# Decay attention and mixer on one core: the first channel group's outputs of batch 2 by seven products

## The chip, the cores and the metric

The kernel runs on one core of one Trainium2 chip. The metric is the device time of one execution in microseconds (us). The engines are TensorE (PE in the profile; its weight loads are PEld), VectorE (DVE), ScalarE (ACT), GpSimd (POOL) and SyncE (SP), which here only issues DMAs.

## The reference

`x` is the output of a block-wise decay attention (4 batches, 8 heads, 768 positions, 64 dims per head; blocks of 64), laid out as 4 x 768 x 512. A mixer follows, and only its second half, the channel mixer, is touched by the change:

```python
xt = x.transpose(0, 2, 1)
h = np.maximum(xt @ w_tok1, 0.0) @ w_tok2
u = x + h.transpose(0, 2, 1)
h2 = np.maximum(u @ w_ch1, 0.0) @ w_ch2      # w_ch1 512 x 1536, w_ch2 1536 x 512
return (u + h2)
```

All is fp32. The weights arrive as 8-byte floats and are narrowed on the chip. Each fp32 operand of a product is held as a high part in a rounded fp32 form that the matmul takes, and a low part that is the rest. A product of two operands is three matmuls: high by high, low by high and high by low.

## The kernel before

**Channel groups and units.** The 1536 hidden channels are cut into six groups of 256 (`NG = 6`, `g` from 0 to 5). A unit is one group for one batch; there are 24, numbered by `n`. Units 0 to 11 do batches 0 and 1 with the groups going up, units 12 to 23 do batches 2 and 3 with the groups going down. Two of the last are swapped (L775), so the last four are: unit 20 = group 1, batch 2; unit 21 = group 0, batch 2; unit 22 = group 1, batch 3; unit 23 = group 0, batch 3. In this text a unit's *pass* is the call `run(n, ...)`, which issues the hidden products of unit n together with the output products of unit n - 1.

**Hidden products.** For a unit, the 256 x 512 weights times the 512 x 768 batch is done by seven block products in place of eight, m1 to m7, each of six matmuls (two row tiles by the three high and low terms) that stream 384 columns. Two functions do this. `mixing` (L809) ends in the four hidden blocks 11, 12, 21, 22 after the relu, each split in a high and a low part. `mixing_seven` (L866) forms, beside blocks 11, 22 and 21, four sums and differences T1 to T4 of hidden blocks, and splits all seven; these are the operands of an output by seven products. Its last pieces (`rest[n]`, function `u`, L931) run in the next pass, behind m1.

**Output products.** `out_pair` (L1014) does a quarter of a unit's output by plain block products, 12 matmuls; four of them, 48 matmuls, make a unit's output, and four DVE additions of 128 x 768 put it into the batch's tile `uT`. `out_seven` (L968) does a unit's output by seven products M1 to M7 of six matmuls, 42 in all, each followed by a DVE addition of 128 x 768 into `uT`. M1, M6, M7 and M4 accumulate one after another in one pair of PSUM banks, M5, M3 and M2 in another; so each of M6, M7, M4, M3 and M2 starts only when the addition of the one before it in its pair is done.

**Weights of the output by seven.** `out_seven` needs seven combinations of the four blocks of the group's w_ch2 rows. `load_sums(g)` (L944) brings the group's fp32 w_ch2 (512 KB) from a copy in DRAM, and `sum_steps(g)` (L952) makes the combinations: four splits (ACT rounds the high part, POOL subtracts for the low part) and four DVE additions of 128 x 256. The fp32 copies in DRAM are written while groups 1 to 4 first pass (`save_c2`). Of group 0, `save(0)` has stored all six tiles, the high and the low part of its w_ch2 among them (`saved[0][4]` and `saved[0][5]`), and `restore(0, 1)` (L1087) brings these two back for `out_pair`.

**Which unit does what.** `SEVEN` (L777) lists the units that use `mixing_seven` and `out_seven`: units 14 to 20 and 22. Group 0 is left out, so units 21 and 23 use `mixing` and `out_pair`.

**What sets the order.** The order on every engine is the order in which the program issues. `run` goes through a list of slots (`SLOTS_OF`, L1107 on) and between slots issues side work that `background(n)` lists with due times: a slot of a product counts 6, a slot of an `out_pair` 12, so a pass is 84 to 90 long. The side work in question is the loading of sums, the sum steps, the restoring of weights, and `store(b, x)` (L1028): one quarter of a batch's output, two DVE transposes of 128 x 384 into a tile `y`, and eight DMAs of 48 KB on SP's queue. Each engine takes its instructions strictly in order, so an instruction that waits holds all that stand behind it.

**The end.** After pass 23 come `out_pair(23, 0)` and `out_pair(23, 1)`, two stores of batch 3 by DVE transposes (tile `ylast`, 14 DMAs on SP's queue and two on ACT's), and four last sums (`last_sum`) whose blocks PE transposes back (`finish`, L1049) and ACT's queue stores in three DMAs of 384, 192 and 192 KB.

Of the kernel before, what the change touches and what calls it, by code (L numbers as in the profile page):

```python
# [22 lines left out]
def kernel(  # L23
# [750 lines left out]
    units = [(g, b) for g in range(NG) for b in (0, 1)] + [(g, b) for g in reversed(range(NG)) for b in (2, 3)]  # L774
    units[-3], units[-2] = units[-2], units[-3]  # L775
    NU = len(units)
    SEVEN = [n for n in range(FIRST, NU - 1) if units[n][0] > 0]  # L777
    hs = {}
    scratch, rest = {}, {}
    late = {}  # L780
# [163 lines left out]
    def load_sums(g):  # L944
        pool, tag = (upool, "uT0") if g == NG - 2 else (hidp, "hh0")
        late["raw", g] = pool.tile([P, JG * DM], U32, tag=tag, name=f"sums_raw{g}")
        nc.sync.dma_start(out=sum_raw(g), in_=saved_c2[g])

    def sum_raw(g):
        return late["raw", g]  # L950
# [77 lines left out]
    def store(b, x, between=None):  # L1028

        sh, t = x // 2, 2 * (x % 2)  # L1030
        k = 2 * b + sh
        y = ytags[0]
        ytags.rotate(-1)
        if isinstance(y, str):
            y = hidp.tile([P, 1024], F32, tag=y, name=f"y{k}{t}")
        y = y[:, : 2 * SB]
        y = y.rearrange("p (blk t q) -> p blk t q", t=2, q=32)
        ub = uT[b][:, t : t + 2, sh * SB : (sh + 1) * SB]
        to = out[b, sh * SB : (sh + 1) * SB].rearrange("(blk s) (t q c) -> q s blk t c", s=32, t=4, q=4)
        for tt in (t, t + 1):  # L1040
            nc.vector.transpose(out=y[:, :, tt - t, :], in_=ub[:, tt - t])
            if between and tt == t:
                between()
        for m in range(4):
            for tt in (t, t + 1):
                eng = nc.scalar if k == LAST - 1 and tt == 3 and m >= 2 else nc.sync
                eng.dma_start(out=to[m, :, :, tt], in_=y[m * 32 : (m + 1) * 32, :, tt - t])
# [39 lines left out]
    def restore(g, x):  # L1087
        if x == 0:
            weights[g] = group_tiles(f"r{g}", g % 2, c2=False)
        else:  # L1090
            both = c2_tile(f"r{g}", g % 2)
            weights[g] += [both[:, 0], both[:, 1]]
        for y in range(6)[4 * x : 4 + 2 * x]:
            nc.sync.dma_start(out=flat(weights[g][y]).bitcast(F32), in_=saved[g][y])
# [19 lines left out]
    def background(n):  # L1114
# [4 lines left out]
        def add(when, *fs):  # L1119
            ev.extend((when, f) for f in fs)  # L1120
# [17 lines left out]
        if 1 < n < NP1 - 1:  # L1138
            to = g + 1
            if n % 2 == 0:  # L1140
                if n == 2:
                    pc = piece_steps(2)
                    add(6, *pc, lambda: fetch(2, 0), split_c2(weights[1], 2, narrowed[2]))
                pa = piece_steps(3)
                add(12, pa[0], pa[1], pa[2])
                add(24, pa[3], pa[4])
                if n < NP1 - 2:
                    add(24, lambda: fetch(to, 1))
                add(36, split_c2(weights[g], 3, narrowed[3]))
                if g < NG - 1:  # L1150
                    add(48, lambda: save_c2(g))
                if n < NP1 - 2:
                    pb = piece_steps(0)
                    weights[to] = group_tiles(to, to % 2)
                    steps["c1"] = c1 = split_c1(weights[to], narrowed[0], narrowed[1], nc.vector)
                    add(36, pb[0])
                    add(48, pb[1], pb[2])
                    add(72, pb[3], pb[4], lambda: fetch(to, 2))
                    add(84, c1[0])
            else:  # L1160
                c1, pa, pb = steps["c1"], piece_steps(1), piece_steps(2)
                add(6, pa[0], pa[1], pa[2])
                add(12, pa[3], pa[4], c1[1], lambda: fetch(to, 3))
                add(36, c1[2], c1[3], c1[4], c1[5], c1[6])
                add(48, c1[7], pb[0], pb[1], pb[2])
                add(72, pb[3], pb[4], split_c2(weights[to], 2, narrowed[2]))
                if to < NG - 1:
                    add(72, lambda: fetch(to + 1, 0))
                if to - 1 < NG - 2:
                    add(84, lambda: save(to - 1))  # L1170
# [42 lines left out]
        if n == FIRST:  # L1213
# [1 line left out]
            add(6, ss[0], ss[1])  # L1215
            add(48, *ss[2:7])
            add(60, ss[7])
        if FIRST <= n < NU - 5 and n % 2 == 0:
            add(84, lambda: load_sums(g - 1))
        if FIRST < n <= NU - 4:  # L1220
            if n % 2:
                late["steps"] = ss = sum_steps(g - 1)
                add(48, ss[0], ss[1])
            else:
                ss = late["steps"]
                add(36, *ss[2:7])
                add(42, ss[7])
        if n >= NU - 2:
            x = 2 * (n - NU + 2)
            add(36, lambda: store(2, x))  # L1230
            add(84, lambda: store(2, x + 1))
        if n >= NP1 + 2 and n % 2 == 0 and n // 2 - NG <= NG - 2:
            nxt = g - 1
            add(6, lambda: restore(nxt, 0))
        if n == NU - 3:
            add(12, lambda: restore(0, 1))
        return deque(sorted(ev, key=lambda x: x[0]))

    second = {}
# [70 lines left out]
```

## Time and profile before

| what | value |
|---|---|
| time before | 563.82 us median of 3 runs (563.75 to 564.18) |
| the profiled execution's own time | 563.57 us |
| span in its profile | 561.6 us, mean granted TensorE clock 0.995 |
| PE busy | 544.1 us, 97% of the span |
| DVE, POOL, ACT busy | 433.4, 271.6, 244.2 us |
| pass 20 (units 20 and 19) | 483.90 to 498.59 us |
| pass 21 | 498.59 to 513.31 us |
| pass 22 | 513.31 to 529.18 us |
| pass 23 | 529.18 to 543.90 us |
| outputs of unit 23 and the last stores | 543.90 to 561.6 us |

The passes' limits are the starts of the first matmul of each m1. A row of the profile's timeline gives start, length, engine, line of the kernel, operation, output <- inputs, shapes and count, and in brackets how long the engine stood idle before it and what ended that. Rows with SPq or ACTq are the issuing of DMAs; the lists of DMAs give size and the time from issue to landing. Matmuls overlap, so their spacing, not the 0.34 us of one, is what one costs.

### The profile page before, as it was taken

The numbers are of one execution on the slowest core, as the hardware profiler recorded it, in microseconds if no ns is written. First come the engines' busy times: TensorE is split into PE (matmuls) and PEld (weight loads), VectorE is DVE, ScalarE is ACT, GpSimd is POOL, SyncE is SP. The second block draws the span as 40 slices with busy tenths as digits, with TensorE's granted clock in tenths as the row PEclk, the third lists the DMA queues.
The fourth block names the chain that finished last, engine by engine and source line by source line (L and its number), as shares of the span: only waits on it lengthen the run. The fifth ranks groups of instructions, "written<-read, shape, count | busy, mean of one in ns | idle before, by whom it ended". The sixth has DMA issues, their size and how long they took to land.

```text
span 561.6 us, 10781 instructions
## 1 busy us (share of the span) xinstructions
PE 544.1 (97%) x4186; PEld 529.2 (94%) x4186; DVE 433.4 (77%) x650; ACT 244.2 (43%) x490; POOL 271.6 (48%) x248
## 2 busy tenths in 40 slices
PE   5999998999999999999999999999999999999994
PEld 4888887999999999999999999999999999999994
DVE  4786789598787989887878887888678777785683
ACT  3564442336253554343444344353455545442421
POOL 5666452557214464443444454453466656662330
PEclk9999999999999999999999999999999999999998
DMA  9998999999102433351725300015864131320337
GB/s 185 253 205 198 211 166 182 188 190 155 28 2 82 176 119 131 104 215 40 246 73 210 109 1 1 0 29 75 212 113 136 57 114 57 113 76 0 45 49 133
DMA packets 176019, 65.72 MB, mean 117 GB/s; under 512 B 163552, under 2 KB 166752, under 8 KB 175968
## 3 DMA queue, kind: packets, MB, share of 16 engines
q1 hardware_dynamic: 172224, 63.75, 47.8%
q10 hardware_dynamic: 3744, 1.28, 0.9%
q8 instruction: 33, 0.54, 0.4%
q14 instruction: 18, 0.15, 0.1%
HBM read 48.24 MB, written 16.78 MB: 116 GB/s over the span
## 4 chain that ended last, share of the span: by engine, by line
PE 82%; DVE 6%; SPq 5%; DMA 4%; ACT 1%; issue 1%; DVEq 0%; ACTq 0%
PE po L1007 23%; PE pa L794 12%; PE pc L794 9%; PE pb L794 7%; PE pa L981 6%; PE pc L981 5%; PE ph L451 4%; PE pd L794 3%; SPq L111 3%; PE sc L299 2%; PE xT L323 2%; DMA vn<-in_v_dram 2%; PE pu L488 2%; PE pu L471 1%; PE xT L333 1%
## 5 line engine op out<-in xcount | busy, mean ns | idle before, releaser
L1022 DVE TENSOR_TENSOR uT<-po,uT 128x768 f32<-128x768 f32 x62 | 58.9, 952 | 22.6 <-PE po L1007 22.3
L286 POOL COPY stb<-sv 64x320 f32<-64x320 f32 x32 | 26.8, 838 | 45.0 <-DVE sv L273 44.1
L805 ACT ACTIVATE c<-c 128x384 f32<-128x384 f32 x42 | 22.1, 526 | 59.2 <-DVE c L850 33.4
L987 DVE TENSOR_TENSOR uT<-pa,uT 128x768 f32<-128x768 f32 x32 | 30.6, 956 | 11.0 <-PE pa L981 10.3
L323 PE MATMUL xT<-a,vn 128*64 128x128 f32 x384 | 35.7, 277 | 0.0
L340 ACT COPY uT<-xT 128x384 f32<-128x384 f32 x32 | 15.3, 478 | 46.2 <-PE xT L333 46.2
L807 POOL TENSOR_TENSOR h22l<-c,h22h 128x384 fp32r<-128x384 f32 x14 | 14.4, 1030 | 41.6 <-ACT h22h L806 41.6
L307 DVE TENSOR_TENSOR a<-sc,mask 128x768 f32<-128x768 f32 x32 | 29.0, 948 | 5.1 <-PE sc L299 5.1
L333 PE MATMUL xT<-qs,stb 128*64 128x128 f32 x320 | 31.3, 273 | 0.0
L987 DVE TENSOR_TENSOR uT<-pc,uT 128x768 f32<-128x768 f32 x24 | 22.9, 955 | 10.6 <-PE pc L981 10.6
L375 POOL TENSOR_TENSOR c1l<-cs,c1h 128x512 fp32r<-128x512 f32 x15 | 19.2, 1292 | 23.2 <-ACT c1h L374 23.2
L451 PE MATMUL ph<-xhi,w1h 128*128 128x256 f32 x96 | 28.2, 294 | 1.3 <-DVE sv L273 0.9
L1007 PE MATMUL po<-h12h,c 128*128 128x384 f32 x112 | 28.7, 337 | 0.0
L1007 PE MATMUL po<-h11h,c 128*128 128x384 f32 x112 | 28.6, 336 | 0.0
L1007 PE MATMUL po<-h21h,c 128*128 128x384 f32 x112 | 28.6, 336 | 0.0
L1007 PE MATMUL po<-h22h,c 128*128 128x384 f32 x112 | 28.6, 336 | 0.0
L451 PE MATMUL ph<-xhi,w1l 128*128 128x256 f32 x96 | 27.1, 282 | 0.0
L451 PE MATMUL ph<-xlo,w1h 128*128 128x256 f32 x96 | 27.1, 282 | 0.0
L299 PE MATMUL sc<-qT,kT 64*128 64x128 f32 x384 | 26.4, 285 | 0.2 <-ACT qT L237 0.2
L299 PEld LDWEIGHTS sc<-qT,kT 64*128 64x128 f32 x384 | 23.4, 192 | 3.3 <-issue 1.8
L364 DVE TENSOR_TENSOR xlo<-xp,xhi 128x384 fp32r<-128x384 f32 x32 | 17.6, 552 | 11.2 <-ACT xhi L363 11.0
L252 POOL TENSOR_TENSOR qs<-qT,lamp 128x640 f32<-128x640 f32 x16 | 25.2, 1577 | 0.3
(401 smaller groups left out, 1928.8 us busy)
## 6 DMA issues: line engine op xcount, KB each, us to landing
raw<-in_moe_w_ch_dram SPq DMA_DIRECT2D x20, 512.0 KB, 3.8
vn<-in_v_dram SPq DMA_DIRECT2D x16, 384.0 KB, 5.2
kn<-in_k_dram SPq DMA_DIRECT2D x30, 192.0 KB, 5.4
out_dram<-y SPq DMA_DIRECT2D x96, 48.0 KB, 1.9
qn<-in_q_dram SPq DMA_DIRECT2D x44, 96.0 KB, 3.9
kr<-in_k_dram SPq DMA_DIRECT2D x32, 96.0 KB, 2.8
dc1h<-c1h SPq DMA_DIRECT2D x4, 768.0 KB, 5.4
dc1l<-c1l SPq DMA_DIRECT2D x4, 768.0 KB, 6.8
```

The costliest lines, as they stand in the source:

```text
L252: nc.gpsimd.tensor_mul(out=qss[i], in0=qTs[i][:, P:].rearrange("p (c i) -> p c i", i=P), in1=lamp[:, p, None, :].broadcast_to([P, NC - 1, P]),
L286: nc.gpsimd.tensor_copy(out=st[r, :, h, :], in_=sv[r].rearrange("p (e c) -> p c e", c=NC - 1))
L299: nc.tensor.matmul(out=sc[h][:, c * P : (c + 1) * P], lhsT=kTs[i][r, cs], rhs=qTs[i][r, cs], start=True, stop=True,)
L307: nc.vector.tensor_mul(out=a, in0=pair.rearrange("p h (c i) -> p h c i", i=P), in1=mask[:, 2 * p : 2 * p + 2, None, :].broadcast_to([P, 2, ...
L323: nc.tensor.matmul(out=xT[h * D : (h + 1) * D, cs], lhsT=vns[i][:, h, c, :], rhs=weights_of[i, g, h][:, cg, :], start=(cg == 0), stop=False,)
L333: nc.tensor.matmul(out=xT[h * D : (h + 1) * D, cs], lhsT=st[:, c - 1, h, :], rhs=qss[i][:, c - 1, :], start=False, stop=(cg == 2),)
L451: nc.tensor.matmul(out=ph, lhsT=w[:, c, fs], rhs=x[:, c], start=(i == 0), stop=(i == 3 * NC - 1))
L794: nc.tensor.matmul(out=to, lhsT=w[:, t], rhs=x[:, t], start=(start and i == 0), stop=(i == 5), skip_group_check=not start,)
L981: nc.tensor.matmul(out=pair[x][:, t], lhsT=w[:, t], rhs=h, start=(start and i == 0), stop=(i == 2), skip_group_check=not start,)
L987: nc.vector.tensor_add(out=ub, in0=pair[x], in1=ub)
L1007: nc.tensor.matmul(out=to, lhsT=w[:, jj, t * P : (t + 1) * P], rhs=h, start=(i == 0), stop=(i == 3 * JG - 1))
L1022: nc.vector.tensor_add(out=ub, in0=po, in1=ub)
```

## The change

Unit 21 joins the units that work by seven products (`SEVEN` is now units 14 to 22). Its hidden products go through `mixing_seven`, its output, in pass 22, through `out_seven`.

The combinations of group 0's w_ch2 need its fp32 values, of which no copy is kept. `load_sums(0)` loads the stored high and low parts, 512 KB each, and a new step `whole` adds them on DVE (128 x 1024). In pass 21 stand `whole` and all four splits and four additions of the sum steps. The high and low parts themselves are still wanted for unit 23, and `restore(0, 1)` moves from pass 21 to pass 23, since its tile now holds the low parts of group 0's combinations until pass 22 is over. Batch 2's four stores change order and place: the two quarters of its second half go first, in pass 22, and the two of its first half follow in pass 23, earlier in the pass than the two that stood there.

```diff
-    SEVEN = [n for n in range(FIRST, NU - 1) if units[n][0] > 0]
+    SEVEN = range(FIRST, NU - 1)
...
     def load_sums(g):
         pool, tag = (upool, "uT0") if g == NG - 2 else (hidp, "hh0")
         late["raw", g] = pool.tile([P, JG * DM], U32, tag=tag, name=f"sums_raw{g}")
-        nc.sync.dma_start(out=sum_raw(g), in_=saved_c2[g])
+        if g == 0:
+            late["lows"] = hidp.tile([P, JG * DM], F32, tag="hl0", name="sums_lows")
+            nc.sync.dma_start(out=sum_raw(0).bitcast(F32), in_=saved[0][4])
+            nc.sync.dma_start(out=late["lows"], in_=saved[0][5])
+        else:
+            nc.sync.dma_start(out=sum_raw(g), in_=saved_c2[g])
+
+    def whole():
+        raw = sum_raw(0).bitcast(F32)
+        nc.vector.tensor_add(out=raw, in0=raw, in1=late["lows"])
...
-        if FIRST <= n < NU - 5 and n % 2 == 0:
+        if FIRST <= n < NU - 3 and n % 2 == 0:
             add(84, lambda: load_sums(g - 1))
+        if n == NU - 3:
+            ss = sum_steps(g)
+            add(6, whole, ss[0], ss[1])
+            add(48, *ss[2:7])
+            add(60, ss[7])
...
         if n >= NU - 2:
-            x = 2 * (n - NU + 2)
-            add(36, lambda: store(2, x))
-            add(84, lambda: store(2, x + 1))
+            x, when = ((2, (48, 72)), (0, (12, 48)))[n - NU + 2]
+            add(when[0], lambda: store(2, x))
+            add(when[1], lambda: store(2, x + 1))
...
-        if n == NU - 3:
-            add(12, lambda: restore(0, 1))
+        if n == NU - 1:
+            add(6, lambda: restore(0, 1))
```

A condition on `save_c2` gains a `0 <`; the step it guards was never reached for group 0.

The order on DVE where pass 20 goes over into pass 21, before. `uT_63` and `uT_62` are the tiles of batches 3 and 2, `pa` and `pc` PSUM banks, `scratch_*` fp32 temporaries of the hidden products; L987 is the addition behind an output product, L924 and L933 are the last differences of the unit before:

```order
L987 TENSOR_TENSOR uT_63<-pa_5611,uT_63 128x2x384
L924 TENSOR_TENSOR scratch_c<-scratch_c,scratch_a_4711 128x384
L933 TENSOR_TENSOR t_20_5768<-scratch_d,scratch_c 128x384
L987 TENSOR_TENSOR uT_62<-pa_5759,uT_62 128x2x384
L832 TENSOR_TENSOR scratch_b_4716<-pb_5788,scratch_a_4712 128x384
L987 TENSOR_TENSOR uT_62<-pc_5758,uT_62 128x2x384
```

And now (L996 is the former L987, L956 is `whole`):

```order
L996 TENSOR_TENSOR uT_63<-pa_5611,uT_63 128x2x384
L924 TENSOR_TENSOR scratch_c<-scratch_c,scratch_a_4711 128x384
L933 TENSOR_TENSOR t_20_5775<-scratch_d,scratch_c 128x384
L956 TENSOR_TENSOR sums_raw_5755<-sums_raw_5755,sums_lows 128x1024
L996 TENSOR_TENSOR uT_62<-pa_5766,uT_62 128x2x384
L894 TENSOR_TENSOR scratch_a_4712<-pb_5797,scratch_a_4712 128x384
L996 TENSOR_TENSOR uT_62<-pc_5765,uT_62 128x2x384
```

`whole` stands between the last difference of unit 20 and the addition behind M1 of pass 21.

The end of SP's queue, before (`y` are the stores of batch 2, `c2r` the restored parts of group 0's w_ch2, `ylast` the stores of batch 3):

```order
L1094 DMA c1hr_5633<-dc1h_2728 128x1536
L1094 DMA c1lr_5634<-dc1l_2729 128x1536
L1094 DMA c2r_5785<-dc2h_2730 128x1024
L1094 DMA c2r_5785<-dc2l_2731 128x1024
L1047 DMA out_dram<-y_5942 32x12x32 x8
L1047 DMA out_dram<-y_6020 32x12x32 x8
L1047 DMA out_dram<-y_6100 32x12x32 x8
L1047 DMA out_dram<-y_6184 32x12x32 x8
L1047 DMA out_dram<-ylast_6195 32x12x32 x14
```

And now:

```order
L1103 DMA c1hr_5633<-dc1h_2728 128x1536
L1103 DMA c1lr_5634<-dc1l_2729 128x1536
L949 DMA sums_raw_5755<-dc2h_2730 128x1024
L950 DMA sums_lows<-dc2l_2731 128x1024
L1056 DMA out_dram<-y_5985 32x12x32 x8
L1056 DMA out_dram<-y_6030 32x12x32 x8
L1103 DMA c2r_6082<-dc2h_2730 128x1024
L1103 DMA c2r_6082<-dc2l_2731 128x1024
L1056 DMA out_dram<-y_6092 32x12x32 x8
L1056 DMA out_dram<-y_6149 32x12x32 x8
L1056 DMA out_dram<-ylast_6219 32x12x32 x14
```

The two loads for `whole` take the restored parts' place, and the restored parts come between the two stores of pass 22 and the two of pass 23.

On PE, behind m1 of pass 22, stood the first of 48 matmuls by `out_pair`; there stands M1 now, six of the 42 by `out_seven`. Before, and now:

```order
L1007 MATMUL po_5901<-h11h_5809,c2r_5785 128x384 x2
L1007 MATMUL po_5901<-h11l_5810,c2r_5785 128x384
L1007 MATMUL po_5901<-h21h_5862,c2r_5785 128x384 x2
L1007 MATMUL po_5901<-h21l_5863,c2r_5785 128x384
L1007 MATMUL po_5901<-h11h_5809,c2r_5785 128x384 x2
```

```order
L990 MATMUL pa_5909<-h11h_5806,sums_5764 128x384
L990 MATMUL pa_5909<-h11h_5806,c2s_5762 128x384
L990 MATMUL pa_5909<-h11l_5807,sums_5764 128x384
L990 MATMUL pa_5909<-h11h_5806,sums_5764 128x384
L990 MATMUL pa_5909<-h11h_5806,c2s_5762 128x384
L990 MATMUL pa_5909<-h11l_5807,sums_5764 128x384
```

In pass 22 the operands are now `sums` and `c2s`, the high and low combinations that pass 21 makes, where they were the restored parts `c2r`.

More of the change, by code (lines that the diff above doesn't have):

```diff
@@ L1149, in background @@
                 add(36, split_c2(weights[g], 3, narrowed[3]))
-                if g < NG - 1:
+                if 0 < g < NG - 1:
                     add(48, lambda: save_c2(g))
```

## The prediction

> **What bounds the kernel now.** I read the page's share of busy time first, then the busy time by pass, then the end of the span.
>
> ```profile
> PE 544.1 (97%) x4186; PEld 529.2 (94%) x4186; DVE 433.4 (77%) x650; ACT 244.2 (43%) x490; POOL 271.6 (48%) x248
> ```
>
> Busy time of each engine by pass (PE, PEld, DVE, ACT, POOL with their counts, then granted clock, DMA share, GB/s), for passes 20 to 23 and the rest:
>
> ```profile
> 483.90:498.59 14.69, 14.69 (x85) 14.69 (x85) 11.85 (x19) 7.65 (x18) 9.45 (x9) 1.00 0.29 107
> 498.59:513.31 14.72, 14.72 (x85) 14.72 (x85) 11.09 (x16) 5.42 (x13) 6.99 (x7) 1.00 0.21 73
> 513.31:529.18 15.87, 15.87 (x91) 15.87 (x91) 8.17 (x12) 5.14 (x11) 3.20 (x4) 1.00 0.18 26
> 529.18:543.90 14.72, 14.72 (x85) 14.72 (x85) 12.16 (x19) 5.45 (x12) 6.81 (x7) 1.00 0.37 54
> 543.90:561.60 17.70, 10.41 (x61) 9.32 (x60) 8.47 (x14) 2.21 (x5) 1.02 (x1) 0.84 0.64 112
> ```
>
> PE is busy through all four passes without a gap at a granted clock of 1.00, so what PE has to do sets the time up to 543.90, and DVE, the next, has 2.5 to 7.7 us to spare in a pass. The last stretch is another matter: PE is busy for 10.4 of 17.7 us. The issues and landings there, first SP's queue, then DVE's transposes for its last two stores, then the last DMA of either queue with its time to landing, then what closes the program:
>
> ```profile
> 537.17 3.94 SPq L1047 DMA_DIRECT2D out_dram<-y  x8
> 545.57 4.82 SPq L1047 DMA_DIRECT2D out_dram<-y  x8
> 550.49 8.76 SPq L1047 DMA_DIRECT2D out_dram<-ylast  x14
> ...
> 547.21 1.04 DVE L1041 STREAM_TRANSPOSE ylast<-uT 128x384 f32<-128x384 f32 x2
> 549.33 0.58 DVE L1041 STREAM_TRANSPOSE ylast<-uT 128x384 f32<-128x384 f32 x1
> 550.28 0.56 DVE L1041 STREAM_TRANSPOSE ylast<-uT 128x384 f32<-128x384 f32 x1
> ...
> 558.75 0.49 SPq L1047 DMA_DIRECT2D out_dram<-ylast  x1
> out_dram<-ylast SPq DMA_DIRECT2D x1, 48.0 KB, 1.9
> 555.75 0.38 ACTq L1067 DMA_DIRECT2D out_dram<-ylast  x1
> out_dram<-ylast ACTq DMA_DIRECT2D x1, 192.0 KB, 2.9
> ...
> L1306 SPq DRAIN  x3: 7/7/7, 560.9 to 561.2; - x3
> ```
>
> SP's last DMA lands at 558.75 + 1.9 = 560.65, ACT's at 555.75 + 2.9 = 558.65; SP drains at 560.9, 0.95 us after its last landing the span is over. So SP's queue ends the kernel, 2.0 us behind ACT's, though the page's chain of waits follows PE and DVE to 555.7. And SP is late because it is still issuing batch 2's last quarter: its eight DMAs run from 545.57 to 550.39, and batch 3's first transpose is ready near 547.21 + 0.58 = 547.8.
>
> **The change part by part.** *PE.* Unit 21's hidden products stay seven of six matmuls. Its output falls from 48 to 42. What six matmuls cost, from the chain of waits:
>
> ```profile
> 538.81 1.05 PE pa L981 x6
> ```
>
> So -1.05 us in pass 22, all of it on the path.
>
> *The loads for `whole`.* They take the place of the restored parts, the same two 512 KB copies, of which the profile has issue and time to landing. They wait for tile `hh0`, that is for POOL's last reading of group 1's sums:
>
> ```profile
> 498.61 0.32 SPq L1094 DMA_DIRECT2D c2r<-dc2h  x1
> 498.97 0.43 SPq L1094 DMA_DIRECT2D c2r<-dc2l  x1
> c2r<-dc2l SPq DMA_DIRECT2D x1, 512.0 KB, 4.4
> 493.33 2.55 POOL L375 TENSOR_TENSOR c2s<-sums_raw,sums_odd 128x512 fp32r<-128x512 f32 x2 [2.27 <-ACT sums_odd L374]
> ```
>
> POOL is through at 495.88, the second load is issued 0.36 us later and lands 4.4 us after that, near 500.65. Group 0's other weights stand ahead of them on SP's queue and went out by 483.9, so nothing holds them; behind them stand only pass 22's stores, not due before 520.
>
> *`whole` and the lock.* DVE reaches `whole` when L933 ends. What is around it on DVE and POOL, and PE's M6 of pass 21:
>
> ```profile
> 500.32 0.56 DVE L933 TENSOR_TENSOR t<-scratch_d,scratch_c 128x384 f32<-128x384 f32 x1
> 500.92 0.96 DVE L987 TENSOR_TENSOR uT<-pa,uT 128x768 f32<-128x768 f32 x1
> 500.84 1.02 POOL L884 TENSOR_TENSOR late_t<-scratch_c,late_t 128x384 fp32r<-128x384 f32 x1 [1.10 <-ACT late_t L883]
> 501.82 1.02 POOL L884 TENSOR_TENSOR h21l<-scratch_d,h21h 128x384 fp32r<-128x384 f32 x1
> 503.86 0.34 PE L981 MATMUL pa<-late_t,sums_odd 128*128 128x384 f32 x1
> ...
> 491.26 0.41 DVE L548 TENSOR_TENSOR sums_raw<-sums_raw 128x256 f32<-128x256 f32 x1
> ```
>
> 128 x 256 takes 0.41 us, 128 x 384 0.56: 0.15 for 128 more, so 128 x 1024 comes to 0.56 + 5 x 0.15 = 1.3 us. Taken alone that would end at 502.2, M1's addition at 503.1, and M6 at 503.86 would not notice. But DVE operations with both inputs in SBUF do not run beside POOL's subtractions:
>
> ```profile
> 526.96 1.01 POOL L884 TENSOR_TENSOR h22l<-scratch_c,h22h 128x384 fp32r<-128x384 f32 x1 [4.29 <-ACT h22h L883]
> 527.42 0.97 DVE L919 TENSOR_TENSOR scratch_a<-scratch_b,scratch_a 128x384 f32<-128x384 f32 x1 [0.66 <-ACT scratch_b L916]
> ...
> 412.33 1.01 POOL L884 TENSOR_TENSOR late_t<-scratch_c,late_t 128x384 fp32r<-128x384 f32 x1 [1.04 <-ACT late_t L883]
> 412.58 1.18 DVE L933 TENSOR_TENSOR t<-scratch_d,scratch_c 128x384 f32<-128x384 f32 x1
> 413.31 1.33 POOL L884 TENSOR_TENSOR h21l<-scratch_d,h21h 128x384 fp32r<-128x384 f32 x1
> ```
>
> L919 ends 0.42 us after POOL does, whenever it started; so does L933, and there the POOL operation behind it waits in turn. One at a time, then, in turns, the blocked one 0.14 us shorter than usual from the release. POOL's L884 starts at 500.84, a hair ahead of `whole`: `whole` runs from 501.86 to about 503.0, M1's addition, which stands behind it, to 503.9, and M6 stands at the edge: a stall of 0 to 0.15 us. If `whole` wins the race instead, none.
>
> [...]
>
> *The other sum steps.* Four DVE additions (4 x 0.42) and four POOL subtractions join pass 21, which on DVE goes from 11.1 to about the 11.85 us of pass 20 plus 1.3. Pass 20 has the same additions and two of the splits, and PE has no gap there, so their bare time is covered. They stand behind M3's addition now, where pass 20 has them ahead of it in 1.1 us of idle time, so DVE's L919 (497.55 in pass 20, 512.3 one pass on) may come as late as 513.2. There the lock adds a second delay: POOL's last sums subtraction, put off like its operands, falls on L919, and T1's subtraction on L924. A meeting costs DVE at most one POOL operation, 1.0 to 1.3 us (2.55 for two above). Behind L924 stand the cast of T2 on ACT and, in ACT's strict order, the copy of m1's bank for which m6 of the next pass waits. In pass 20 these are
>
> ```profile
> 485.97 0.47 ACT L889 COPY scratch_a<-pa 128x384 f32<-128x384 f32 x1
> 488.10 0.34 PE L794 MATMUL pa<-T2h,c1hr 128*128 128x384 f32 x1
> ```
>
> 1.7 us of air. A lateness of 0.9 and one whole meeting, 2.2, overruns it by 0.5; a second of half the length makes 1.0. With the 0.15 at M6, PE's stalls in passes 21 and 22 lie between 0, if POOL and DVE hardly meet, and 1.2 us. I take 0.4, one meeting of less than full length. PE then gains 1.05 - 0.4 = 0.65 us.
>
> The cover of the new ACT casts (four of 0.4 to 0.6 us) is ACT's idle half; without it they would cost 2.2.
>
> *The stores.* In pass 22 and 23 batch 2's quarters leave earlier. The last, due at 48 of 84, gives SP its eight DMAs near 538, as the store at 537.17 above, done by about 543. SP is then free when batch 3's transposes come. These stay tied to PE's output products, so they come 0.65 us sooner: first transpose done at 547.21 + 0.58 - 0.65 = 547.1. With the pace of today, 8.76 us for 14 issues, the last DMA starts 0.49 before 555.9 and lands at 557.3. ACT's chain, moved by 0.65 only, lands at 558.0, and becomes the end. Its last 192 KB took 2.9 us amid SP's issues (the one before 3.6). With SP through by then it will be shorter; loads of 128 KB took 2.0 to 2.5 us in this kernel, by these rows:
>
> ```profile
> a11hr<-da11h SPq DMA_DIRECT2D x1, 128.0 KB, 2.0
> a11hr<-da11h SPq DMA_DIRECT2D x1, 128.0 KB, 2.5
> ```
>
> Bounds 2.1 and 3.6; I take 2.5, which is -0.4.
>
> The restored parts, now behind M4 of pass 22 (near 528), land under 5 us later by the rows above, 9 us ahead of their use at about 543; pass 23's stores, queued behind them, are due after 531. DVE's transposes in passes 22 and 23 are the same eight, and these passes have DVE room as the table shows (8.2 and 12.2 of 15); three more additions of 0.96 bring pass 22 to about 13 of 14.7.
>
> *The sum*, on the profiled execution's own 563.57: PE -0.65; the end from SP's queue to ACT's, 560.65 to 558.65, -2.0; the shorter last landing -0.4. That is 560.5. The median of the runs stands 0.25 above the profiled execution, so **560.8 us**.
>
> **The rivals.** *Late `whole`.* If the second load lands after 501.8, POOL's next subtraction gets in first and `whole` ends a further 1.0 us later; M6 stalls by 1.0 to 1.2 and PE gains nothing. For it: the margin is 1.1 us on a landing of 4.4. Against: the same copies, in as idle a stretch. The end still gains 2.0 to 2.4: 561.4 to 562.
>
> *The end stays.* If the DMA engines, not SP's issuing, pace the last stores, moving the stores ahead frees nothing. For it: the DMA share of 0.64 over the last stretch, issues that stretch from 0.49 to over 0.6 us. Against: before 545.57 SP and DMAs stand idle again, and the eight issues at 537.17 went out at 0.49 each. Only PE's 0.65 would be left: 563.2.
>
> *No lock at this place.* `whole` wins its race and POOL and DVE pass each other: the whole 1.05, 560.4.
>
> *Slower.* `whole` waits at the head of DVE's queue, so every us by which its loads land after 501.8 goes to PE. It costs 1:1, and has to eat 1.05 + 2.4 and 1.1 more to be seen as a loss: a landing after 506, some 10 us after the issue, against 4.4 for its like. The time would be 565 or more.
>
> That the change doesn't do what it says is ruled out by the order, six matmuls fewer on PE.
>
> **How the numbers follow.** Forecast 0.72, no lock 0.06, late `whole` 0.11, the end stays 0.08, slower 0.03. The forecast's own ends: stalls 0 and landing 2.1 give 563.57 + 0.25 - 1.05 - 2.0 - 0.8 = 560.0; stalls 1.2 and landing 3.2 (nearly the mean of 2.9 and 3.6) give 563.57 + 0.25 + 0.15 - 2.0 + 0.3 = 562.3. With a little below for SP's and ACT's ends that I place to 0.1 or 0.2 only: 559.8 to 562.3, which holds the late case too. A change under 0.2%, 1.1 us, can't be told from none here: faster 0.89, same 0.08, slower 0.03.
>
> **What would show it.** Right: M1 to M7 of pass 22 in place of 48 L1007 matmuls; `whole` near 1.1 us past POOL's L884, or 2.1 long with the wait counted; PE gaps in passes 21 and 22 of 0.2 to 0.6 us in sum; SP's `ylast` issues from about 547 without a stretch of `y` ahead; the last landing ACT's. Wrong: a wait of `whole` on a DMA; 14 issues that take over 9 us; a gap ahead of unit 23's outputs for the restored parts.

## The result, and the profile after

The changed kernel takes 561.21 us (median of 5 runs, 560.80 to 561.38) against 563.82 before: a ratio of 0.9949, 95% interval 0.9937 to 0.9961. The forecast was 560.8 with a range of 559.8 to 562.3. The profiled execution has a time of its own of 561.38 us and a span of 559.5, where before it was 563.57 and 561.6.

The page of the changed kernel, busy time of the engines, six PE instructions fewer:

```profile
PE 542.8 (97%) x4180; PEld 527.9 (94%) x4180; DVE 439.2 (78%) x659; ACT 248.3 (44%) x500; POOL 281.5 (50%) x256
```

Busy time by pass in the changed kernel, for passes 21, 22 and 23 and the rest (PE, PEld, DVE, ACT, POOL with their counts, granted clock, DMA share, GB/s):

```profile
498.58:513.30 14.72, 14.72 (x86) 14.72 (x85) 12.37 (x19) 7.92 (x18) 11.42 (x11) 1.00 0.11 42
513.30:528.08 14.78, 14.78 (x86) 14.65 (x85) 12.56 (x19) 6.40 (x14) 8.66 (x8) 1.00 0.12 17
528.08:542.80 14.72, 14.72 (x86) 14.72 (x86) 13.29 (x21) 5.88 (x13) 6.99 (x7) 1.00 0.79 151
542.80:559.50 16.70, 10.41 (x61) 9.32 (x60) 7.53 (x12) 2.21 (x5) 1.01 (x1) 0.90 0.58 106
```

Pass 22 takes 14.78 us where it took 15.87, and the last stretch 16.70 where it took 17.70. These two, 1.09 and 1.00, are the 2.1 us between the spans of these two executions. Pass 21, which now has `whole` and the sum steps, is as long as before, and POOL's work in it grew from 6.99 to 11.42 us.

`whole` (L956) and its neighbours, first on DVE, then on POOL:

```profile
500.31 0.56 DVE L933 TENSOR_TENSOR t<-scratch_d,scratch_c 128x384 f32<-128x384 f32 x1
500.78 1.22 DVE L956 TENSOR_TENSOR sums_raw<-sums_raw,sums_lows 128x1024 f32<-128x1024 f32 x1
501.92 0.95 DVE L996 TENSOR_TENSOR uT<-pa,uT 128x768 f32<-128x768 f32 x1
...
500.82 2.06 POOL L884 TENSOR_TENSOR late_t<-scratch_c,late_t 128x384 fp32r<-128x384 f32 x1 [1.10 <-ACT late_t L883]
```

In this execution `whole` waits for no DMA and runs at once, 1.22 us. POOL's subtraction is the one that is held: 2.06 us where the like took 1.02. M1's addition (L996), one input of which is in PSUM, takes its usual 0.95 us beside the second half of that.

The two later meetings of DVE and POOL in passes 21 and 22, and the only gap of PE there:

```profile
508.07 0.95 DVE L548 TENSOR_TENSOR sums_raw<-sums_raw 128x256 f32<-128x256 f32 x1
513.03 0.56 DVE L919 TENSOR_TENSOR scratch_a<-scratch_b,scratch_a 128x384 f32<-128x384 f32 x1
513.62 1.54 DVE L921 TENSOR_TENSOR scratch_b<-scratch_c,scratch_b 128x384 f32<-128x384 f32 x1
...
507.72 1.02 POOL L884 TENSOR_TENSOR h11l<-scratch_a,h11h 128x384 fp32r<-128x384 f32 x1
513.09 1.65 POOL L375 TENSOR_TENSOR c2s<-sums_raw,sums 128x512 fp32r<-128x512 f32 x1
...
517.50 0.42 PE L794 MATMUL pa<-T2h,c1hr 128*128 128x384 f32 x1
517.76 0.34 PE L794 MATMUL pa<-T2h,c1lr 128*128 128x384 f32 x1
```

L548 lasts 0.95 instead of 0.41, L921 1.54 instead of 0.56: DVE loses 0.54 and 0.98 us. On PE the second matmul of m6 starts 0.26 us after the first, where 0.175 is the usual spacing, so 0.08 us is all that reaches it.

The end: SP's issues of batch 3 as one stretch, then its second and its last issue alone, then ACT's last, the landings of the last of either queue, and the close of SP's program:

```profile
546.72 10.60 SPq L1056 DMA_DIRECT2D out_dram<-ylast  x14
547.17 1.91 SPq L1056 DMA_DIRECT2D out_dram<-ylast  x1
556.84 0.47 SPq L1056 DMA_DIRECT2D out_dram<-ylast  x1
554.64 0.44 ACTq L1076 DMA_DIRECT2D out_dram<-ylast  x1
out_dram<-ylast SPq DMA_DIRECT2D x1, 48.0 KB, 1.9
out_dram<-ylast ACTq DMA_DIRECT2D x1, 192.0 KB, 3.3
L1320 SPq DRAIN  x3: 7/7/7, 558.8 to 559.1; - x3
```

SP has no `y` left when batch 3 begins, and starts at 546.72 instead of 550.49. But its 14 issues take 10.60 us instead of 8.76, one of them 1.91. Its last DMA lands at 556.84 + 1.9 = 558.74, ACT's at 554.64 + 3.3 = 557.94. SP still ends the kernel, by 0.8 us instead of 2.0.

### The profile page after: what moved, and what is told of

It is laid out like the page before. It is cut to its first block, busy times and chain, and to the rows that moved or that the text cites. A ratio compares the mean times of both kernels' runs of the same rounds, so it can differ in the third digit from the quotient of the medians.

```text
span 559.5 us, 10806 instructions
## 1 busy us (share of the span) xinstructions
PE 542.8 (97%) x4180; PEld 527.9 (94%) x4180; DVE 439.2 (78%) x659; ACT 248.3 (44%) x500; POOL 281.5 (50%) x256
## 4 chain that ended last, share of the span: by engine, by line
PE 82%; DVE 7%; SPq 4%; DMA 3%; ACT 2%; issue 1%; DVEq 0%; ACTq 0%
PE po L1016 22%; PE pa L794 12%; PE pc L794 9%; PE pb L794 7%; PE pa L990 7%; PE pc L990 5%; PE ph L451 4%; PE pd L794 3%; SPq L111 3%; PE sc L299 2%; PE xT L323 2%; PE pu L488 2%; PE xT L333 2%; PE pu L471 1%; DMA qn<-in_q_dram 1%
## 5 line engine op out<-in xcount | busy, mean ns | idle before, releaser
L1031 DVE TENSOR_TENSOR uT<-po,uT 128x768 f32<-128x768 f32 x58 | 55.2, 952 | 17.4 <-PE po L1016 17.1
L996 DVE TENSOR_TENSOR uT<-pa,uT 128x768 f32<-128x768 f32 x36 | 34.4, 954 | 11.0 <-PE pa L990 10.3
L996 DVE TENSOR_TENSOR uT<-pc,uT 128x768 f32<-128x768 f32 x27 | 25.8, 954 | 12.0 <-PE pc L990 12.0
```

The source lines that it names most:

```text
L996: nc.vector.tensor_add(out=ub, in0=pair[x], in1=ub)
L1031: nc.vector.tensor_add(out=ub, in0=po, in1=ub)
```

## The experiments

**Which part brings the time.** The change without its earlier stores in pass 23:

```diff
-            x, when = ((2, (48, 72)), (0, (12, 48)))[n - NU + 2]
+            x, when = ((2, (48, 72)), (0, (36, 84)))[n - NU + 2]
```

> The changed kernel with batch 2's two stores of pass 23 back at the times they had before (36 and 84 in place of 12 and 48). Theory A, SP's queue sets the end and the moved stores freed it: the last eight DMAs of batch 2 run from about 544.5 to 549.3, the 14 issues behind them start near 549.4 instead of 546.7, last landing near 559.7 in place of 558.7, about 1 us slower than the changed kernel, near 562.2. Theory B, the last stores are paced by the DMA engines and their start does not matter: as the changed kernel, near 561.2.

Measured: 562.71 us, ratio 0.9976 (0.9967 to 0.9985). The other way round, the kernel before with the stores of pass 23 at the early places and nothing else:

```diff
-            x = 2 * (n - NU + 2)
-            add(36, lambda: store(2, x))
-            add(84, lambda: store(2, x + 1))
+            x, when = ((0, (36, 84)), (2, (12, 48)))[n - NU + 2]
+            add(when[0], lambda: store(2, x))
+            add(when[1], lambda: store(2, x + 1))
```

> The kernel before with only the stores of pass 23 moved from 36 and 84 to 12 and 48; unit 21 stays with out_pair. Theory A: PE as before, SP's last 14 issues start near 547.8 instead of 550.5 and take 8.8 to 10.6 us, ACT's last landing (558.65) is the floor; 0.9 to 2.0 us off, 561.8 to 562.9. Theory B: no change, 563.8.

Measured: 562.61 us, ratio 0.9974 (0.9963 to 0.9984). The parts bring 0.24% and 0.26% and add up to the 0.51% of the whole. So about half of the gain is the six matmuls and half the stores; the profile's 1.09 and 1.00 say the same. Both runs speak for theory A: where the stores move and where they don't, the time follows, and the 561.2 and 563.8 of theory B lie outside.

**The same kernel once more.** No edit; it stands beside the runs with the large memset, with ACT's share in the kernel before and with 12 unused matmuls below.

> The changed kernel once more, as the comparison for the three others on this chip: ratio near 0.995.

Measured: 561.12 us, ratio 0.9951 (0.9939 to 0.9964). Its profiled execution is a quicker one, 560.59 us with a span of 558.8. Its last stretch, SP's issues, the landings of the last DMAs of SP's and ACT's queue, and SP's close:

```profile
542.90:558.80 15.90, 10.41 (x61) 9.34 (x60) 7.53 (x12) 2.22 (x5) 1.01 (x1) 0.93 0.60 110
546.82 8.76 SPq L1056 DMA_DIRECT2D out_dram<-ylast  x14
out_dram<-ylast SPq DMA_DIRECT2D x2, 48.0 KB, 3.0
out_dram<-ylast ACTq DMA_DIRECT2D x1, 192.0 KB, 2.9
...
L1320 SPq DRAIN  x3: 7/7/7, 558.0 to 558.3; - x3
```

PE's part is the same to 0.1 us, but the last stretch takes 15.90 instead of 16.70 with the same code, because the 14 issues took 8.76 us this time. So the end of this kernel differs by 0.8 us between these two executions, and the pace of SP's issues is what differs.

**Who ends the kernel.** In the changed kernel, four more of the 48 KB DMAs of the last two stores go to ACT's queue:

```diff
-                eng = nc.scalar if k == LAST - 1 and tt == 3 and m >= 2 else nc.sync
+                eng = nc.scalar if k == LAST - 1 and tt != 2 and m >= 2 else nc.sync
```

> The changed kernel with four of the eight DMAs of batch 3's first store by transposes issued on ACT's queue, so that SP has 10 last issues, not 14. Theory A (issuing on SP sets the end, 0.8 us behind ACT's last landing): SP's last landing comes about 2 us earlier, ACT's near 557.9 is the end; 0.8 us faster than the changed kernel, near 560.4. Theory B (the DMA engines pace the last stores): within 0.3 us of 561.2.

> The kernel of e4 once more, beside the two others: 560.2 to 560.6, and about 0.2 to 0.5 us below or above e10_last_piece as that run's theories say.

Measured: 560.37 us, ratio 0.9933 (0.9919 to 0.9946), and in the second run 560.85, ratio 0.9932 (0.9908 to 0.9955). In the first run's profile SP has issued all by 552.99, ACT's last DMA is the end, and the program closes 1.2 us earlier than in the changed kernel's first profile, 0.4 earlier than in its second:

```profile
546.82 6.17 SPq L1056 DMA_DIRECT2D out_dram<-ylast  x10
554.75 0.38 ACTq L1076 DMA_DIRECT2D out_dram<-ylast  x1
out_dram<-ylast ACTq DMA_DIRECT2D x1, 192.0 KB, 2.8
L1320 SPq DRAIN  x3: 7/7/7, 557.6 to 557.9; - x3
```

So SP's queue did set the end in the profiles of the change, by 0.8 and 0.3 us. Both ratios lie 0.2% below those of the change (0.9949 and 0.9951), which makes this the quickest version, though the intervals overlap. The second run's 560.85 us is above what was expected; the kernel before took 564.29 beside it, and the ratio is the same.

With ACT's queue the end, its last 192 KB still took 2.8 us (3.1 in the second run's profile), with SP silent. The DMA engines were not silent. The first row is of 548 to 551 us in the changed kernel, the other two of that stretch and of the end in the first run with ACT's share (the last two numbers are the busy share of the DMA engines and GB/s):

```profile
548.00:551.00 3.00, 3.00 (x19) 2.63 (x18) 2.14 (x6) 0.20 (x1) 0.00 (x0) 1.00 0.35 52
548.00:551.00 3.00, 3.00 (x19) 2.56 (x18) 2.24 (x5) 0.17 (x1) 0.00 (x0) 1.00 0.98 129
553.00:557.00 4.00, 0.52 (x3) 0.31 (x3) 0.94 (x2) 0.00 (x0) 0.00 (x0) 1.00 0.92 215
```

From 553 to 557 the share is 0.91 in the changed kernel too, and 1.03 in its second profile (a transfer counts where it starts, so a stretch can pass 1). As these rows read, SP's queue costs time early on, when it leaves the DMA engines 0.35 busy (0.56 in the second profile), while at the end they have little room whoever issues. That part of the rival "the end stays" is true.

The same share in the kernel before:

> The kernel before with four of the eight DMAs of batch 3's first store by transposes issued on ACT's queue, stores of batch 2 and unit 21 as before. Theory A (issuing on SP sets the end): SP has 10 issues behind batch 2's last quarter, about 2 to 3 us less, and ACT's last landing (558.65) becomes the end: 1.5 to 2.0 us faster than the kernel before, ratio 0.9965 to 0.9975. Theory B (DMA engines): within 0.3 us of the kernel before.

Measured: 562.74 us, ratio 0.9980 (0.9970 to 0.9989), 1.1 us. That is less than was expected, since SP still ends there. The row is of its SP queue:

```profile
550.98 7.41 SPq L1047 DMA_DIRECT2D out_dram<-ylast  x10
```

Ten issues that start at 550.98, behind batch 2's last quarter, and run beside ACT's large DMAs take 7.41 us, 0.74 each, and end at 558.4.

The last 192 KB cut in two, 64 KB of it on SP's idle queue:

```diff
-            nc.scalar.dma_start(out=to[:, :, es], in_=ylast[:, :, es])
+            if t == 3:
+                nc.sync.dma_start(out=to[:, 0:1, es], in_=ylast[:, 0:1, es])
+                nc.scalar.dma_start(out=to[:, 1:3, es], in_=ylast[:, 1:3, es])
+            else:
+                nc.scalar.dma_start(out=to[:, :, es], in_=ylast[:, :, es])
```

> The kernel of e4 (the changed kernel with the odd columns' m >= 2 pieces of the last two stores on ACT's queue) with the last piece of the output (192 KB, the last issue on ACT's queue) split by rows: 64 KB of it issued by SP, 128 KB by ACT. In e4 SP's queue has issued all by 552.99 and that last piece, issued at 554.75, ends the kernel, 2.8 us from issue to landing. Theory A (the landing of the last piece goes by its bytes and by what shares its queue): the landing falls to 2.3 to 2.6 us, the time to 559.9 to 560.2. Theory B (what it costs is a fixed latency of a DMA, about 2 us or more whatever its bytes): 560.3 to 560.6, as e4.

Measured: 560.51 us (559.97 to 561.83), ratio 0.9935 (0.9912 to 0.9957), no different from the 560.85 beside it. The landings of the two pieces, and the DMA share at the end (its slowest execution is the profiled one):

```profile
out_dram<-ylast ACTq DMA_DIRECT2D x1, 128.0 KB, 3.7
out_dram<-ylast SPq DMA_DIRECT2D x1, 64.0 KB, 3.3
...
553.00:557.00 4.00, 0.68 (x4) 0.31 (x3) 1.11 (x2) 0.48 (x1) 0.00 (x0) 1.00 1.00 218
```

Each piece landed no sooner than the 2.8 and 3.1 us of the whole, and the time is as theory B had it. But the run doesn't show a fixed latency: the same 192 KB were under way together, and the DMA engines were busy throughout (share 1.00). Which part of a landing is a fixed time and which the other stores' work stays open.

**The race for the lock.** A memset of 128 x 64 ahead of `whole` makes it come a little later; in the second kernel one of 128 x 256:

```diff
     def whole():
         raw = sum_raw(0).bitcast(F32)
+        nc.vector.memset(cp.tile([P, 64], F32, tag="spare", name="spare"), 0.0)
         nc.vector.tensor_add(out=raw, in0=raw, in1=late["lows"])
```

> The changed kernel with a DVE memset of 128 x 64 ahead of the addition of high and low parts, so that POOL's subtraction starts first. Theory lock: the addition now ends near 503.0 (about 2 us with its wait, against 1.22), M1's addition near 503.9, and PE's stalls in passes 21 and 22 sum to 0.2 to 0.6 us where the changed kernel has 0.1; time 561.3 to 561.8. Rival, no lock between this DVE addition and POOL: the addition takes 1.22 us again, only the memset is added, PE as in the changed kernel, 561.2.

> As the kernel with the 128 x 64 memset, with a memset of 128 x 256, so that the addition asks about 0.25 us after POOL's subtraction has begun (0.03 us was not enough to lose the race). Theory lock: the addition of high and low parts ends near 503.0, M1's addition near 503.9, M6 of pass 21 starts 0 to 0.15 us late and PE's stalls in passes 21 and 22 sum to 0.1 to 0.6 us; time 561.2 to 561.8. Rival, no lock: the addition takes 1.22 us and PE is as in the changed kernel.

Measured: 561.07 us, ratio 0.9946 (0.9933 to 0.9958), with the small one, and 561.32, ratio 0.9956 (0.9942 to 0.9970), with the large one. With the small one `whole` still went first, though POOL's subtraction has the earlier start in the record:

```profile
500.95 1.17 DVE L957 TENSOR_TENSOR sums_raw<-sums_raw,sums_lows 128x1024 f32<-128x1024 f32 x1
...
500.92 2.08 POOL L884 TENSOR_TENSOR late_t<-scratch_c,late_t 128x384 fp32r<-128x384 f32 x1 [1.10 <-ACT late_t L883]
```

This run did not make the case it was to make. With the large one `whole` loses; PE's rows are of M6 of pass 21:

```profile
501.33 1.87 DVE L957 TENSOR_TENSOR sums_raw<-sums_raw,sums_lows 128x1024 f32<-128x1024 f32 x1
503.12 0.94 DVE L997 TENSOR_TENSOR uT<-pa,uT 128x768 f32<-128x768 f32 x1
...
501.10 1.02 POOL L884 TENSOR_TENSOR late_t<-scratch_c,late_t 128x384 fp32r<-128x384 f32 x1 [1.10 <-ACT late_t L883]
502.08 2.01 POOL L884 TENSOR_TENSOR h21l<-scratch_d,h21h 128x384 fp32r<-128x384 f32 x1
...
504.12 0.44 PE L991 MATMUL pa<-late_t,sums_odd 128*128 128x384 f32 x1
504.40 0.34 PE L991 MATMUL pa<-late_t,c2s 128*128 128x384 f32 x1
```

Losing the lock costs `whole` 0.65 us, and PE a spacing of 0.28 instead of 0.175, 0.1 us. The time doesn't tell the two outcomes of the race apart.

The race also falls both ways with no edit there. Six of the profiled kernels have the changed kernel's pass 21 (times in us):

| kernel | second load lands | `whole` starts | POOL's subtraction starts | goes first |
|---|---|---|---|---|
| change | 500.65 | 500.78 | 500.82 | `whole` |
| change, once more | 500.81 | 500.91 | 500.91 | `whole` |
| late stores | 501.07 | 501.17 | 501.00 | POOL |
| ACT's share | 500.94 | 501.03 | 500.90 | POOL |
| ACT's share, once more | 501.38 | 501.48 | 501.49 | `whole` |
| last piece divided | 501.22 | 501.31 | 501.24 | POOL |

In five of them `whole` starts about 0.09 us behind the landing of its second load, in the first 0.13, where DVE was not free sooner. So the landing sets the start of `whole`, and with it who goes first: `whole` where it came 4.40 to 4.47 us after the issue, POOL where it came after 4.54 to 4.64. Where POOL does, M6 of pass 21 has the spacing of 0.28 and the later m6 none over 0.2; where `whole` does, m6 has 0.25 to 0.28. PE loses about 0.1 us either way.

**What stretches SP's issues.** In every profile so far a load of instructions stands beside the longest issue near the end. They come on a queue of their own, 33 loads, 0.54 MB, so 16 KB each (a second such queue, 18 loads with 0.15 MB, has none in the stretches looked at here). In the changed kernel the last falls at 547.18, and SP's issue of 1.91 us starts at 547.17. The row is of the DMA queues in the 1.7 us from 547.0:

```profile
q8 instruction: 1, 0.02, 5.5%
```

To move the loads, 12 small matmuls whose result nobody uses were put at the head of PE's program:

```diff
+    spare = bank("xT", "spare", 3 * P)
+    for x in range(12):
+        nc.tensor.matmul(out=spare[:, 0:32], lhsT=ident, rhs=ident[:, 0:32], start=True, stop=True)
```

> The changed kernel with 12 small matmuls (identity by 32 columns of it, nowhere used) at the head of PE's program, where PE waits for the first loads anyway. They move PE's last load of 16 KB of instructions, which stood at 547.18 and fell on an SP issue of 1.91 us, some 2 to 5 us ahead. Theory instruction load: SP's last 14 issues have no long one near 547, end about 1.4 us earlier, ACT's last landing is the end, 0.5 to 0.8 us faster than the changed kernel. Rival, the long issue has another cause (the first issue behind a pause, say): it is there again at the same place, no change in time.

Measured: 562.11 us, ratio 0.9969 (0.9957 to 0.9980), slower than the change, against what was expected. The trace shows two opposite effects. The last instruction load moved to 545.26, when SP has nothing to issue, and the 14 issues of `ylast` went out without a long one at their head:

```profile
548.09 8.49 SPq L1059 DMA_DIRECT2D out_dram<-ylast  x14
```

That unused PE matmuls move the loads shows that they are PE's. Counted from the start of pass 23, the kernel ends 0.8 us earlier than the changed one in its first profile (560.1 - 529.46 = 30.6 against 31.4), but no earlier than in its second (558.8 - 528.18 = 30.6), so a gain in time from the moved load is not shown. And the load that stood at 502.20 moved to 499.34, into the landing of the second load for `whole`. The rows are the two loads with their time to landing, `whole`, and PE's M6 of pass 21:

```profile
sums_raw<-dc2h SPq DMA_DIRECT2D x1, 512.0 KB, 3.7
sums_lows<-dc2l SPq DMA_DIRECT2D x1, 512.0 KB, 5.9
...
502.62 1.65 DVE L959 TENSOR_TENSOR sums_raw<-sums_raw,sums_lows 128x1024 f32<-128x1024 f32 x1 [1.39 <-DMA sums_lows<-dc2l]
...
505.19 0.44 PE L993 MATMUL pa<-late_t,sums_odd 128*128 128x384 f32 x1 [0.82 <-DVE uT L999]
...
498.95:514.77 15.82, 15.00 (x86) 14.68 (x86) 12.84 (x20) 8.24 (x19) 11.88 (x11) 1.00 0.10 38
```

The second load lands 5.9 us after its issue instead of 4.4, `whole` waits 1.39 us for it, and pass 21 takes 15.82 us instead of 14.72. Of the sixteen completions that the copy reports, fifteen had come by 501.06; the last came at 502.53. With the 0.37 us by which the unused matmuls delay pass 21's start, 0.37 + 1.10 - 0.09 (pass 22) - 0.78 gives the 0.6 us between this span and that of the changed kernel's first profile. This is the rival "late `whole`", brought about by the place of an instruction load.

To see whether that meeting is the cause, the same kernel with the loads for `whole` due earlier:

```diff
-            add(84, lambda: load_sums(g - 1))
+            add(60 if n == NU - 4 else 84, lambda: load_sums(g - 1))
```

> The kernel of e7 (the changed kernel with 12 small unused matmuls at the head of TensorE) with the two loads for `whole` moved from slot 84 to slot 60 of unit 20, some 4 us earlier on SP's queue. In e7 the trace shows an instruction load of 16 KB at 499.34, while the second load for `whole` was still landing (5.9 us from issue to landing instead of 4.4), `whole` waiting 1.39 us for it and TensorE 0.97 us at M1 of pass 21. Theory A (e7's loss of about 0.9 us against the changed kernel comes from that meeting of the two loads): here the loads land before the instruction load begins, `whole` starts at about 501 as in the changed kernel, the stall of pass 21 shrinks to 0.1 or less, pass 23 starts about 528.5 instead of 529.46, SP's 14 last issues still take about 8.5 us (no instruction load beside them), and the time is 561.0 to 561.4. Theory B (the unused matmuls themselves, or something else late, cost e7 its time): 561.9 to 562.3 as e7.

Measured: 562.15 us, ratio 0.9962 (0.9949 to 0.9975), as before the edit. But the edit moved nothing: the loads were issued at 496.43 and 496.79, behind a wait on SP for the tile that POOL still read:

```profile
SPq L952 <- POOL c2s L375: 12.0, 1, 12.0
```

So the run repeats the last one (landing 6.0 us, wait 1.47, pass 21 15.82) and says nothing on the cause. In its place, 36 unused matmuls instead of 12, to move the load away from the landing:

```diff
-    for x in range(12):
+    for x in range(36):
```

> The kernel of e7 with 36 instead of 12 small unused matmuls at the head of TensorE. In the changed kernel an instruction load of 16 KB falls at 502.20, 12 matmuls moved it to 499.34 and the work itself by 0.37 us; 36 would move the work by about 1.1 us and the load to about 493.6 (and the ones after it to about 515 and 539), ahead of the two loads for `whole` (their issues about 497.0 and 497.4). Theory A (e7's stall at pass 21 comes from that instruction load, which falls on the landing of the second load for `whole`): here the second load lands 4.4 to 4.7 us after its issue instead of 5.9, `whole` waits for no DMA, pass 21 takes 14.7 to 14.8 us instead of 15.8, and SP's 14 last issues, with no instruction load beside them, take 8.3 to 8.8 us; the time is 561.5 to 562.0. Theory B (the stall has another cause that any unused matmuls bring): the second load takes 5.5 us or more again, pass 21 takes 15.8 and the time is 562.6 to 563.2.

Measured: 571.34 us, ratio 1.0129 (1.0113 to 1.0146). The expected time was far off, and neither theory is to be judged by it: the unused matmuls take 0.43 us each, not the few hundredths I had taken from the 0.37 us by which twelve delayed the work. Twelve were nearly hidden, since the first data arrive at 5.34 us; 36 are not:

```profile
1.34 15.57 PE L643 MATMUL spare<-ident 128*128 128x32 f32 x72 [1.34 <-POOL ident masks.py:199]
```

What was to be told apart shows in the trace all the same. Everything stands 10.85 us later (pass 21 starts at 509.43), and the instruction loads fall at 499.92, 523.56 and 548.49, none of them on the loads for `whole` or on SP's last issues:

```profile
509.43:524.26 14.83, 14.83 (x85) 14.66 (x85) 13.30 (x19) 8.03 (x18) 11.53 (x11) 1.00 0.11 42
sums_lows<-dc2l SPq DMA_DIRECT2D x1, 512.0 KB, 4.5
511.68 2.10 DVE L959 TENSOR_TENSOR sums_raw<-sums_raw,sums_lows 128x1024 f32<-128x1024 f32 x1
557.59 8.30 SPq L1059 DMA_DIRECT2D out_dram<-ylast  x14
```

The landing is back at 4.5 us, `whole` waits for no DMA (its 2.10 us are a lost race with POOL, whose subtraction of 1.03 us starts at 511.68 as well), pass 21 takes 14.83, and the 14 issues 8.30. That is theory A in each of these points: with more unused matmuls than before the stall is gone, so it was not they that made it. What stays of pass 21's growth, 0.1 us, is the lost race.

All the profiles together, the 14 issues of `ylast` on SP's queue and the place of the last instruction load (the kernels with ACT's share issue ten there and are left out):

| kernel | load at | what SP issues then | 14 issues, us |
|---|---|---|---|
| before | 548.31 | `y`, one of 1.36 | 8.76 |
| change | 547.18 | `ylast`, one of 1.91 | 10.60 |
| change, once more | 547.46 | `ylast`, one of 1.12 | 8.76 |
| late stores | 547.57 | `y`, one of 1.55 | 9.07 |
| stores alone | 549.17 | `ylast`, one of 1.53 | 9.85 |
| small memset | 547.60 | `ylast`, one of 1.25 | 9.45 |
| large memset | 547.66 | `ylast`, one of 1.61 | 10.05 |
| 12 unused matmuls | 545.26 | nothing | 8.49 |
| the same, loads due earlier | 545.34 | nothing | 8.50 |
| 36 unused matmuls | 548.49 | `y`, one of 1.40 | 8.30 |

Where the load falls on `ylast`, the 14 issues take 8.76 to 10.60 us, 9.7 in the mean; elsewhere 8.30 to 9.07, 8.6 in the mean. The two ranges overlap. The long issue near 547 goes where the load goes: that was shown by moving the load. What the two share is not shown. Other long issues, of 0.9 to 1.4 us, stand near the end beside ACT's large DMAs with no instruction load near, in the kernels with moved loads too.

## Why the prediction was right, and where it was wrong

**Six matmuls, -1.05 us.** Pass 22 became 1.09 us shorter. Right.

**The loads, landing near 500.65.** They landed there, and `whole` began at 500.78 without a wait. Right, and the margin of 1.1 us that the rival "late `whole`" was given is as thin as it said: an instruction load in the wrong place used it up, and pass 21 was then 1.1 us longer, where the rival had 1.0 to 1.2. For the race there was no margin: `whole` starts on that landing.

**The race, taken as lost.** In the changed kernel's two profiles it was won, in three of the six with the same pass 21 it was lost. The step that failed is to read the outcome from POOL's recorded start, "a hair ahead of `whole`", in one profile: a landing 0.1 to 0.2 us later turns it, and the landing varies by that much. Its price was sized right: a lost race cost PE 0.1 us, within the 0 to 0.15 of the prediction.

**The stalls, taken as 0.4 of 0 to 1.2.** 0.08 was measured in the first profile, 0.1 in the second. The meetings came as foretold, on L548 and behind L919, but the step "a lateness of 0.9 and one whole meeting, 2.2" was too large. L919 came at 513.03, 0.7 after the 512.3 of an undisturbed pass, and the meeting behind it cost 0.98: 1.7 in all, just the 1.7 us of air. This term was mis-sized by 0.3, on the safe side.

**The end, -2.0 and -0.4.** Here the sum was off. SP was freed as described: its issues began at 546.72, with no `y` before them. "With the pace of today, 8.76 us for 14 issues" held in one profiled execution of the changed kernel and not in the other, where they took 10.60. Then the last landings: SP's last DMA was to land 1.9 us after its issue, ahead of ACT's. In the first execution SP was last, at 558.74, 1.4 us past the 557.3 foretold; "14 issues that take over 9 us" was one of the prediction's own signs of being wrong. In the second, with the pace of 8.76, SP's last two landed 3.0 us after their issue (median), beside ACT's 192 KB, and the program closed at 558.0, still 0.8 earlier than in the first. And the shorter landing of ACT's last 192 KB, 2.5 us, was not found: 3.3 and 2.9 in the two executions, 2.8 and 3.1 where SP had nothing left to issue. The step that failed is "With SP through by then it will be shorter". By the prediction's own times SP's last issue (555.4) comes after ACT's (0.65 before 555.75), and even where SP was through, the DMA engines were 0.92 busy from 553 to 557. The 128 KB loads that the 2.5 was taken from were no guide to a store there. The end from the start of pass 23 shrank by 1.0 us in the first execution and 1.8 in the second, where 2.4 was taken.

**The restored parts, near 528.** They were issued at 533.21 and 533.67, behind the 16 DMAs of pass 22's stores, and the second landed 5.0 us later, at 538.7. That is 4 us ahead of their use instead of 9, still no gap on PE.

**The sum.** In the profiled executions' own times 3.05 us were foretold and 2.19 came: 0.45 more from PE, 1.4 less from the end, 0.1 outside the spans. That is 561.38 where 560.5 was foretold, 0.9 off. The median of 561.21 is only 0.4 above the forecast, since it was to stand 0.25 above the profiled execution and stood 0.17 below; that closeness is in part luck, and so is it that the errors of PE and of the end had opposite signs. The mechanism was right in both parts, PE's six matmuls and SP's queue, as the two halves run alone show. Their shares were not: 0.65 and 2.4 were taken, and about half and half came.

**The rivals.** "The end stays" is not what happened, but its reason is part of the truth: beside the other queue's large DMAs SP's issues do take longer (in the changed kernel 1.27, 0.98 and 1.14 us at 553.31, 554.63 and 555.66, where the eight before took 0.41 to 0.49), and the DMA engines are 0.9 busy or more from 553 to 557. "No lock" had the PE gain right, 1.0 to 1.1 in the two executions, with the lock there all the same. "Slower" was not seen; the latest landing met was 5.9 to 6.0 us after the issue, not 10.

## What to carry to other kernels

When a stretch ends on a queue of many small DMAs, give the pace of its issues a range, not the value of one profiled execution: here 8.3 to 10.6 us for the same 14. Look at where the instruction loads fall before taking a load with 1 us of margin as safe, since twelve matmuls more at the head of PE's program moved them here by 1.9 and 2.9 us (547.18 to 545.26, 502.20 to 499.34). And before pricing a delay on a helper engine as a stall, subtract the air that the consumer still has: two meetings at the lock cost DVE 1.5 us and PE 0.08. A race that 0.1 us decides is priced with both outcomes, not with the one that a single profile shows.

## What the runs showed of the hardware

**Instruction loads are not free for others.** PE's instructions come in 16 KB loads (33 loads, 0.54 MB), about one per 22 us late in this kernel: in the changed kernel at 459.51, 479.89, 502.20, 523.84 and 547.18. PE itself shows no gap there (in passes 20 to 23 of the kernel before, with loads at 502.75 and 523.76, no two of its matmuls start over 0.2 us apart), but in the two kernels with 12 unused matmuls a 512 KB copy under way landed after 5.9 and 6.0 us instead of 4.4 to 4.6, and an issue on SP's queue took 1.1 to 1.9 us instead of 0.3 to 0.5. Not every meeting costs: in the kernel before the load at 502.75 began 0.6 us ahead of such a copy's landing, which came after 4.4 us all the same.

**The record of POOL's start does not say who has the lock.** POOL's subtraction at 500.92 lost against a DVE addition that starts at 500.95 in the record, and one at 511.68 won against a DVE addition of the same start. A difference of 0.03 us does not decide; in the four profiles where POOL's start was ahead by 0.07 us (501.24 against 501.31) to 0.23 (501.10 against 501.33), POOL had the lock.
